# Attention, gated MLP and MLP on one core: both heads' scores of a query tile issued in turn, in the first batch

## The chip, the cores and the metric

The kernel runs on one core of a Trainium2 chip. The metric is the device time of one execution in microseconds (us). Engines are called by their names or as the profile does: PE is TensorE (PEld its weight loads), DVE is VectorE, ACT is ScalarE, POOL is GpSimd, SP is SyncE, which issues most DMAs.

## The reference

Block-causal attention (4 batches, 8 heads, 576 positions, head dimension 64, blocks of 64), then a gated MLP with a spatial product over the positions, then a normalized MLP with a residual. The change lies in the attention's first product, the scores.

```python
scores = scale * np.matmul(q, k.transpose(0, 1, 3, 2))
scores = np.where(mask, scores, -1000000000.0)
attn = np.exp(scores - np.max(scores, axis=-1, keepdims=True))
attn = attn / (np.sum(attn, axis=-1, keepdims=True) + 1e-09)
x = np.matmul(attn, v)
...
h = np.maximum(x @ w_in, 0.0)
...
gated = u * v_s
x = gated @ w_out
...
ch = np.maximum(xn @ w_ch1, 0.0) @ w_ch2
return (x + ch).astype(np.float32)
```

## The kernel before

The attention works on **pairs** of heads, 4 pairs a batch, pairs 0 to 15. A pair is cut into 7 **units** in the order of `UNITS`: the tail (the last 64 query rows of both heads in one tile of 128 rows, `c == 4`), then the query tiles 3, 2 and 1 (128 rows each; tile 1 also takes tile 0 along), each for head 0 and then for head 1. In the text 3/0 is tile 3 of head 0, 3/1 that of head 1, and so on. The main loop (`for u in range(NS + 8)`) takes one unit after another through three stages:

- `scores(u)`: matmuls into a PSUM bank of the pool `p_sc`, which has three banks. q and k are held as a high and a low part that sum to the fp32 value (`stacks`, and `qtail` for the tail). In the first batch (pairs below `PACKED` = 4) head 0 lies on partitions 0 to 63 and head 1 on 64 to 127, and a score is three products over 64 rows: high by high, high by low, low by high. From pair 4 on a score is two products over 128 rows. The first three units (`PLAIN`) take the fp32 operands as they are.
- `softmax(u)`: VectorE adds the mask, takes the minimum and writes the tile `p` to SBUF in one reduction (L322), which frees the score bank; ScalarE does the exponential and the sum (L328). There are six `p` tiles (`pt`) and a single `tail` tile.
- `transposes(u - 2)`: TensorE turns the probabilities, 128 columns at a time (L378), into one of two banks of `p_tr`, and VectorE or ScalarE copies them to `pH` or `pL` (L370, L372).

`weighted` then multiplies with v (pv, L429), in a first half on `pL` and a second one on `pH`; `reciprocals` (rps, L341, and the copy rr, L343) and `store_x` finish a pair. In between stand `prepare` (high and low parts of a later pair: L56 or L58 for the high ones, on GpSimd L233 or L245 and L247 for the low ones), the decoding of w_in (`DECODE`: ACT L88, DVE L89 and L90, POOL L101 and L102) and, from pair 4 on, the first dense matmuls (vps, ups: L106 to L108) which `fill` adds.

The order on each engine is not that of the source: the kernel is built with a scheduler that keeps a time line of its own and moves instructions within what their data allow. `tc.keep_in_program_order` (here `pin`) holds the instructions it is given in the order of the source among themselves. The zero matmuls of `warm` and of `lead` (`ZEROS`) are extra work for TensorE; `lead` writes them into a score bank before the scores.

```python
ZEROS = {NU * p + i: n for p in range(4) for i, n in ((6, 1), (7, 2))}
...
UNITS = [(None, 4)] + [(j, c) for c in (3, 2, 1) for j in range(2)]
...
elif p < PACKED:
    for i, (x, y) in enumerate(((0, 0), (0, 1), (1, 0))):
        MM(out, lhsT=st[rows, x, 0, q], rhs=st[rows, y, 1, 0:nn], start=(i == 0), stop=(i == 2))
```

Of the kernel before, what the change touches and what calls it, by code (L numbers as in the profile page):

```python
# [8 lines left out]
F32 = mybir.dt.float32  # L9
# [24 lines left out]
def tile_kernel(  # L34
# [35 lines left out]
    MM = nc.tensor.matmul  # L70
# [62 lines left out]
    p_sc = tc.alloc_tile_pool(name="p_sc", bufs=PLAN["sc"], space=PSUM, side="right")  # L133
# [7 lines left out]
    PACKED = PLAN['packed']  # L141
# [26 lines left out]
    def pin(ins, on=True):  # L168
        if on:
            tc.keep_in_program_order(ins)  # L170
# [85 lines left out]
    NU = len(UNITS)  # L256
    PLAIN = PLAN['plain']
    state = {}

    sums = {}  # L260

    ZEROS = {NU * p + i: n for p in range(4) for i, n in ((6, 1), (7, 2))}

    def scores(u):
        p = u // NU
        j, c = UNITS[u % NU]

        def lead(ps):
            for _ in range(ZEROS.get(u, 0)):
                MM(ps, lhsT=zeros.to_broadcast([128, 128]), rhs=zeros.to_broadcast([128, 512]), start=True, stop=True)  # L270
        st, qt, _, raw = ops[p]
        banks = []
        plain = u < PLAIN
        if c == 4:
            sums[p] = at.tile([128, 9], F32, tag="sm", name="sm")
            for a, z in ((0, 256), (256, S)):
                s_ps = p_sc.tile([128, 512], F32, tag="sc", name="sc")
                if a == 0:
                    lead(s_ps)
                if plain:  # L280
                    pin(MM(s_ps[:, :z - a], lhsT=last_q, rhs=raw[:, 0, 1, a:z], start=True, stop=True))
                elif p < PACKED:
                    for n, (x, y) in enumerate(((0, 0), (0, 1), (1, 0))):
                        MM(s_ps[:, :z - a], lhsT=qt[:, x, 0, :], rhs=st[:, y, 1, a:z], start=(n == 0), stop=(n == 2))
                else:
                    for h in range(2):
                        for i in range(2):
                            MM(  # L288
                                s_ps[:, :z - a], lhsT=qt[:, i, h, :], rhs=st[:, h, 2, a:z],
                                start=(h == 0 and i == 0), stop=(h == 1 and i == 1),  # L290
                            )
                banks.append((s_ps[:, :z - a], a, z - a))
        else:
            s_ps = p_sc.tile([128, 512], F32, tag="sc", name="sc")
            lead(s_ps)
            rows = slice(64 * j, 64 * j + 64) if j is not None else None
            for a, c in ((0, c),) if c > 1 else ((0, 1), (256, 0)):
                n = 128 * (c + 1)
                out = s_ps[:, a:a + max(n, 192)]
                nn = max(n, 192)  # L300
                q = slice(128 * c, 128 * c + 128)
                if plain:
                    pin(MM(out, lhsT=raw[rows, 0, 0, q], rhs=raw[rows, 0, 1, 0:nn], start=True, stop=True))
                elif p < PACKED:
                    for i, (x, y) in enumerate(((0, 0), (0, 1), (1, 0))):
                        MM(out, lhsT=st[rows, x, 0, q], rhs=st[rows, y, 1, 0:nn], start=(i == 0), stop=(i == 2))
                else:
                    for i in range(2):
                        MM(out, lhsT=st[:, j, i, q], rhs=st[:, j, 2, 0:nn], start=(i == 0), stop=(i == 1))  # L309
                banks.append((s_ps[:, a:a + n], 0 if c != 1 else 128, n))  # L310
        state[u] = banks

    def softmax(u):
# [245 lines left out]
    for u in range(NS + 8):  # L559
        p, i = divmod(u, NU)  # L560
        if u < NS:
            scores(u)
            warm(WARM.get(u, 0))
            softmax(u)
# [624 lines left out]
```

## Time and profile before

| what | value |
|---|---|
| median of 3 runs | 796.72 us (794.71 to 797.81) |
| the profiled execution | 793.98 us |
| its span, first to last instruction | 792.2 us |
| PE busy | 776.4 us, 98% of the span |
| DVE, ACT, POOL busy | 513.9, 428.6, 419.2 us |
| granted TensorE clock, mean | 1.000 |
| units 0 to 27, the first batch | up to about 51.7 us, where the tail scores of pair 4 begin |

A busy time is the union of an engine's instructions. For PE the ends of matmuls are modelled and they overlap, so the step from one start to the next start tells more than a duration. The value in brackets behind a row of the timeline is the engine's idle time ahead of it and what ended it.

### The profile page before, as it was taken

How to read it: one execution, taken by the hardware profiler on the slowest of the kernel's cores; microseconds unless marked ns; L12 is line 12 of the kernel's file. 1: busy time of each engine (PE TensorE's matmuls, PEld its weight loads, DVE VectorE, ACT ScalarE, POOL GpSimd, SP SyncE). 2: the span in 40 equal slices, each digit the busy share in tenths (PEclk: the TensorE clock that was granted, in tenths of full speed). 3: DMA queues.
4: the chain of work that ended last, by engine and by line, in shares of the span. 5: the costliest groups of instructions: out<-in, count | busy, mean ns of one | idle time of the engine just before them, and what ended most of it. 6: DMA issues, size and time to landing. Idle time of an engine off the chain costs nothing.

```text
span 792.2 us, 13259 instructions
## 1 busy us (share of the span) xinstructions
PE 776.4 (98%) x4508; PEld 669.4 (84%) x4508; DVE 513.9 (65%) x1165; ACT 428.6 (54%) x1051; POOL 419.2 (53%) x436
## 2 busy tenths in 40 slices
PE   9999999999999999899999999999999999999997
PEld 5766788778888899789988988889989898898996
DVE  6677756555464457786777788897566588555534
ACT  5888776777654464555444555553354454333421
POOL 5699966675632453232375565465545465545431
PEclk9999999999999999999999999999999999999999
DMA  9866455545332669779420332204010003000002
GB/s 251 206 177 171 126 173 154 154 119 154 96 115 74 197 199 289 224 247 285 135 81 24 110 107 82 80 19 141 1 30 25 0 1 125 23 0 1 1 1 79
DMA packets 53847, 88.70 MB, mean 112 GB/s; under 512 B 6930, under 2 KB 17298, under 8 KB 53780
## 3 DMA queue, kind: packets, MB, share of 16 engines
q1 hardware_dynamic: 53540, 87.55, 37.2%
q8 instruction: 35, 0.57, 0.3%
q10 hardware_dynamic: 240, 0.31, 0.2%
q14 instruction: 32, 0.26, 0.1%
HBM read 68.88 MB, written 18.95 MB: 111 GB/s over the span
## 4 chain that ended last, share of the span: by engine, by line
PE 86%; DVE 6%; DMA 3%; issue 2%; POOL 1%; ACT 1%; SPq 1%; DVEq 0%; ACTq 0%; POOLq 0%
PE hps L968 21%; PE o L106 8%; PE o L107 8%; PE o L108 8%; PE pv L429 6%; PE tr L378 4%; PE sc L309 3%; PE ups L106 2%; PE vps L106 2%; PE ups L108 2%; PE ups L107 2%; PE vps L107 2%; PE vps L108 2%; PE sc L288 2%; PE by L106 2%
## 5 line engine op out<-in xcount | busy, mean ns | idle before, releaser
L102 POOL TENSOR_TENSOR a<-s,a 128x256 fp32r<-128x256 f32 x96 | 78.2, 818 | 91.4 <-ACT a L97 91.4
L107 PE MATMUL o<-w,h 128*128 128x512 f32 x288 | 112.3, 391 | 0.0
L106 PE MATMUL o<-w,h 128*128 128x512 f32 x288 | 107.0, 395 | 1.0 <-ACT h L960 1.0
L974 DVE TENSOR_TENSOR c<-hps,c 128x384 f32<-128x384 f32 x120 | 66.5, 554 | 52.1 <-PE hps L968 50.5
L108 PE MATMUL o<-w,h 128*128 128x512 f32 x288 | 96.5, 394 | 0.3 <-DVE h L961 0.3
L102 POOL TENSOR_TENSOR a<-w,a 128x256 fp32r<-128x256 f32 x72 | 61.5, 856 | 44.3 <-ACT a L97 38.5
L97 ACT CAST a<-s 128x256 fp32r<-128x256 f32 x96 | 38.3, 404 | 83.4 <-PE hps L968 74.9
L328 ACT ACTIVATE p<-p,nm 128x512 f32<-128x512 f32 (+3 forms) x128 | 70.9, 556 | 18.1 <-DVE nm L322 14.5
L322 DVE CUSTOM_DVE_ANT_0 p<-sc,mask 128x512 f32<-128x512 f32 (+3 forms) x128 | 58.3, 484 | 33.2 <-PE tr L378 12.5
L106 PEld LDWEIGHTS o<-w,h 128*128 128x128 f32 x288 | 53.8, 188 | 11.0 <-ACT h L960 2.3
L107 PEld LDWEIGHTS o<-w,h 128*128 128x128 f32 x288 | 54.1, 188 | 9.6
L370 DVE COPY pH<-tr 128x512 f32<-128x512 f32 (+1 forms) x88 | 49.2, 575 | 19.7 <-PE tr L378 19.4
L108 PEld LDWEIGHTS o<-w,h 128*128 128x128 f32 x288 | 53.2, 188 | 8.4 <-DVE h L961 1.2
L818 POOL TENSOR_TENSOR gt<-gf,gt 128x576 fp32r<-128x576 f32 (+1 forms) x17 | 25.0, 1472 | 62.5 <-ACT gt L817 62.5
L378 PE MATMUL tr<-idn,p 128*128 128x128 f32 x320 | 48.8, 276 | 2.1 <-DVE pH L370 1.9
L439 POOL TENSOR_TENSOR xx<-xx,rb 128x576 f32<-128x576 f32 x16 | 22.7, 1421 | 49.1 <-DMA rb<-r_d 40.3
L961 DVE SCALAR_TENSOR_TENSOR h<-c,h 128x384 fp32r<-128x384 f32 x72 | 46.0, 658 | 1.6 <-ACT h L960 1.5
L88 ACT ACTIVATE dm<-raw 128x256 f32<-128x256 f32 (+1 forms) x72 | 31.8, 462 | 27.4 <-DVE w L90 6.3
L378 PEld LDWEIGHTS tr<-idn,p 128*128 128x128 f32 x320 | 36.9, 140 | 10.6 <-DVE pH L370 5.3
L309 PE MATMUL sc<-stack 128*128 128x256 f32 (+2 forms) x192 | 42.7, 338 | 2.9 <-DVE nm L322 2.5
L245 POOL TENSOR_TENSOR stack<-qkt,stack 64x576 fp32r<-64x576 f32 x24 | 34.0, 1417 | 21.4 <-ACT stack L58 15.8
L117 POOL TENSOR_TENSOR rs<-rs,nhalf 128x1 f32<-128x1 f32 x36 | 22.4, 622 | 42.6 <-DVE rs L116 37.0
(188 smaller groups left out, 2270.7 us busy)
## 6 DMA issues: line engine op xcount, KB each, us to landing
raw<-in_w_ch_dram SPq DMA_DIRECT2D x64, 256.0 KB
qkt<-in_qk_dram SPq DMA_DIRECT2D x110, 144.0 KB
vt<-in_v_dram SPq DMA_DIRECT2D x16, 320.0 KB
rb<-r_d SPq DMA_DIRECT2D x32, 144.0 KB
u_d<-ur SPq DMA_DIRECT2D x16, 288.0 KB
us<-u_d SPq DMA_DIRECT2D x16, 288.0 KB
y_d<-ys SPq DMA_DIRECT2D x18, 256.0 KB
yr<-y_d SPq DMA_DIRECT2D x18, 256.0 KB
```

What stands on the lines that cost most here:

```text
L102: {"v": nc.vector, "g": nc.gpsimd}[low].tensor_tensor(lo, src, f32(hi), op=ALU.subtract)
L106: MM(out_ps, lhsT=a[0], rhs=b[0], start=first, stop=False)
L107: MM(out_ps, lhsT=a[0], rhs=b[1], start=False, stop=False)
L108: MM(out_ps, lhsT=a[1], rhs=b[0], start=False, stop=last)
L309: MM(out, lhsT=st[:, j, i, q], rhs=st[:, j, 2, 0:nn], start=(i == 0), stop=(i == 1))
L322: nc.vector.tensor_tensor_reduce(pt[:, o:o + n], src, m, -0.125, nm[:, 0:1] if c == 4 and i == 1 else 3e38, ALU.add, ALU.min, nm[:, i:i + 1],)
L328: nc.scalar.activation(pt[:, o:o + n], pt[:, o:o + n], AF.Exp, bias=nm[:, i:i + 1], scale=-1.0, accum_out=sm[:, col:col + 1])
L370: nc.vector.tensor_copy(out, src)
L378: nc.tensor.transpose(tr[:, o:o + 128], pt[:, 128 * kc:128 * kc + 128], idn)
L429: MM(ps[64 * j:64 * j + 64, a:z], lhsT=vt[:rows, kc, 64 * j:64 * j + 64], rhs=src[:rows, j, w * kc + a:w * kc + z] if part else src[:rows, ...
L968: MM(ps, lhsT=a[x], rhs=b[y], start=not more and kc == 0 and k == 0, stop=kc == KD // 2 - 1 and k == 2, skip_group_check=True,)
L974: nc.vector.tensor_tensor(out, ps, x, op=ALU.add)
```

## The change

In the first batch, behind the three plain units, `scores` is done for both heads of a tile when head 0's unit comes: two banks are taken, one for each head, and the three products are issued in turn, head 0, head 1, head 0 and so on. All but the first of these matmuls are pinned in the source's order. Head 1's unit then finds its state filled and issues no scores. The single zero matmul of `lead` moves from unit 6 (1/1) to unit 5 (1/0) of a pair, so that it comes ahead of tile 1's scores. For the tail, the plain units and the pairs from 4 on the same matmuls are issued as before.

```diff
-    ZEROS = {NU * p + i: n for p in range(4) for i, n in ((6, 1), (7, 2))}
+    ZEROS = {NU * p + i: n for p in range(4) for i, n in ((5, 1), (7, 2))}
...
-            s_ps = p_sc.tile([128, 512], F32, tag="sc", name="sc")
-            lead(s_ps)
...
-                elif p < PACKED:
-                    for i, (x, y) in enumerate(((0, 0), (0, 1), (1, 0))):
-                        MM(out, lhsT=st[rows, x, 0, q], rhs=st[rows, y, 1, 0:nn], start=(i == 0), stop=(i == 2))
...
+            parts = ((0, c),) if c > 1 else ((0, 1), (256, 0))
+            heads = (0, 1) if p < PACKED and not plain else (j,)
+            if j == heads[0]:
+                pss = {h: p_sc.tile([128, 512], F32, tag="sc", name="sc") for h in heads}
+                lead(pss[j])
+                for a, c in parts:
...
+                    terms = ((0, 0), (0, 1), (1, 0)) if p < PACKED else ((0, 2), (1, 2))
+                    for i, (x, y) in enumerate(terms):
+                        for h in heads:
+                            rows = slice(64 * h, 64 * h + 64)
+                            left, right = (st[rows, x, 0, q], st[rows, y, 1, 0:nn]) if p < PACKED else (
+                                st[:, h, x, q], st[:, h, 2, 0:nn])
+                            ins = MM(
+                                pss[h][:, a:a + nn], lhsT=left, rhs=right, start=(i == 0), stop=(i == len(terms) - 1)
+                            )
+                            pin(ins, len(heads) > 1 and (i > 0 or h > 0 or a > 0))
+                for h in heads:
+                    state[u + h - j] = [
+                        (pss[h][:, a:a + 128 * (c + 1)], 0 if c != 1 else 128, 128 * (c + 1)) for a, c in parts
+                    ]
+            return
```

The scheduler makes its order anew from this. The queues of all five engines differ up to the first scores of pair 8 (about 114 us of the profile) and list the same instructions in the same order from there on. In the changed kernel the lines behind the edit are higher by 10: L312 are these scores, L332 the reduction, L380 the pH copy, L388 the transposes, L439 pv.

TensorE in pair 2, tiles 3 and 2, before (sc_501 and sc_525 are the banks of 3/0 and 3/1, sc_551 and sc_567 of 2/0 and 2/1):

```order
L306 MATMUL sc_501<-stack0_89 128x512 x3
L378 MATMUL tr_385<-idn_114,p_330 128x128 x4
L306 MATMUL sc_525<-stack0_89 128x512 x3
L378 MATMUL tr_400<-idn_114,p_354 128x128 x4
L306 MATMUL sc_551<-stack0_89 128x384 x3
L378 MATMUL tr_420<-idn_114,p_380 128x128 x3
L306 MATMUL sc_567<-stack0_89 128x384 x3
```

and with the change (sc_501 and sc_502 are now 3/0 and 3/1, sc_551 and sc_552 2/0 and 2/1):

```order
L312 MATMUL sc_501<-stack0_89 128x512
L312 MATMUL sc_502<-stack0_89 128x512
L312 MATMUL sc_501<-stack0_89 128x512
L312 MATMUL sc_502<-stack0_89 128x512
L312 MATMUL sc_501<-stack0_89 128x512
L312 MATMUL sc_502<-stack0_89 128x512
L388 MATMUL tr_400<-idn_114,p_354 128x128 x4
L388 MATMUL tr_428<-idn_114,p_384 128x128 x3
L312 MATMUL sc_551<-stack0_89 128x384
L312 MATMUL sc_552<-stack0_89 128x384
```

The transposes that stood between two heads of a tile now stand behind both.

TensorE in pair 3 before, from the transposes of pair 2's tail on (sc_676 and sc_703 are the banks of 3/0 and 3/1; pv_544 is the first half of pair 1's pv, on pL):

```order
L378 MATMUL tr_533<-idn_114,tail_122 128x128 x4
L306 MATMUL sc_676<-stack1_90 128x512 x3
L306 MATMUL sc_703<-stack1_90 128x512 x3
L378 MATMUL tr_541<-idn_114,tail_122 128x128
L429 MATMUL pv_544<-pL_363,vt_134 64x256 x2
L429 MATMUL pv_544<-pL_363,vt_134 64x128 x2
```

and with the change (sc_676 and sc_677 are 3/0 and 3/1):

```order
L388 MATMUL tr_533<-idn_114,tail_122 128x128 x4
L312 MATMUL sc_676<-stack1_90 128x512
L388 MATMUL tr_541<-idn_114,tail_122 128x128
L439 MATMUL pv_544<-pL_363,vt_134 64x256 x2
L439 MATMUL pv_544<-pL_363,vt_134 64x128 x2
L312 MATMUL sc_677<-stack1_90 128x512
L312 MATMUL sc_676<-stack1_90 128x512
L312 MATMUL sc_677<-stack1_90 128x512
```

The first matmul of the tile, which is not pinned, stands alone, and other work comes between it and the other five. The same holds for tiles 2 and 1 of this pair.

VectorE in pair 1 before (p_380 and p_396 are the reductions of 2/0 and 2/1, p_414 the first one of 1/0, dm and de the decoding of w_in, rr the copy of the reciprocals):

```order
L89 TENSOR_SCALAR de_254<-raw_170 128x512
L322 ISA p_380,nm_381<-sc_376,mask_119 128x384
L322 ISA nm_381 128x1
L89 TENSOR_SCALAR de_342<-raw_172 128x512
L90 SCALAR_TENSOR_TENSOR dm_253<-dm_253,de_254 128x512
L343 COPY rr_317<-rps_315 9x128
L322 ISA p_396,nm_397<-sc_392,mask_119 128x384
L322 ISA nm_397 128x1
L322 ISA p_414,nm_415<-sc_407,mask_119 128x256
```

and with the change (p_384, p_396 and p_422 are the same three reductions):

```order
L89 TENSOR_SCALAR de_262<-raw_170 128x512
L90 SCALAR_TENSOR_TENSOR dm_261<-dm_261,de_262 128x512
L89 TENSOR_SCALAR de_346<-raw_172 128x512
L353 COPY rr_317<-rps_315 9x128
L332 ISA p_384,nm_385<-sc_376,mask_119 128x384
L332 ISA nm_385 128x1
L332 ISA p_396,nm_397<-sc_377,mask_119 128x384
L332 ISA nm_397 128x1
L380 COPY pH_364<-tr_358 128x4x2x64
L90 SCALAR_TENSOR_TENSOR dm_345<-dm_345,de_346 128x512
L332 ISA p_422,nm_423<-sc_407,mask_119 128x256
```

The first L90 and the copy rr now stand ahead of both reductions of tile 2, and the pH copy and the second L90, which stood behind the reductions of tile 1, ahead of them.

## Rows read from the trace of the kernel before

**Rows 1.** The page, part 4: the chain of waits by engine, over the whole span.
```profile
PE 86%; DVE 6%; DMA 3%; issue 2%; POOL 1%; ACT 1%; SPq 1%; DVEq 0%; ACTq 0%; POOLq 0%
```

**Rows 2.** Windows cut at the first scores of pairs 2, 3 and 4.
```profile
core 0: us, PE busy (x) PEld busy (x) DVE busy (x) ACT busy (x) POOL busy (x), PEclk, DMA share, GB/s
...
25.10:37.50 12.40, 12.40 (x82) 8.26 (x81) 8.44 (x27) 8.97 (x31) 9.08 (x10) 1.00 0.95 221
37.50:51.70 14.20, 13.39 (x93) 9.40 (x91) 10.41 (x30) 12.26 (x32) 13.75 (x14) 1.00 0.64 175
```

**Rows 3.** Timeline of PE in pair 2: start, us, engine, line, operation, count.
```profile
27.98 0.66 PE L378 MATMUL tr<-idn,p 128*128 128x128 f32 x4
28.57 0.96 PE L306 MATMUL sc<-stack 64*128 64x512 f32 x3
29.46 0.66 PE L378 MATMUL tr<-idn,p 128*128 128x128 f32 x4
...
30.77 0.55 PE L378 MATMUL tr<-idn,p 128*128 128x128 f32 x3
...
31.96 0.55 PE L378 MATMUL tr<-idn,p 128*128 128x128 f32 x3
...
36.40 0.93 PE L306 MATMUL sc<-stack 64*128 64x256 f32 x6
37.27 0.61 PE L270 MATMUL sc<-const-float32-0.0 128*128 128x512 bf16 x2
```

**Rows 4.** Timeline of PE: a lone score matmul (pair 1), and eight transposes unbroken (pair 4).
```profile
22.42 0.55 PE L378 MATMUL tr<-idn,p 128*128 128x128 f32 x3
22.90 0.35 PE L306 MATMUL sc<-stack 64*128 64x192 f32 x1
23.18 0.39 PE L270 MATMUL sc<-const-float32-0.0 128*128 128x512 bf16 x1
...
55.41 1.03 PE L378 MATMUL tr<-idn,p 128*128 128x128 f32 x8
56.20 0.59 PE L309 MATMUL sc<-stack 128*128 128x384 f32 x2
```

**Rows 5.** Timeline of PE in pair 1: 3/0 and 3/1 together.
```profile
17.16 0.97 PE L306 MATMUL sc<-stack 64*128 64x512 f32 x6
18.06 0.55 PE L378 MATMUL tr<-idn,p 128*128 128x128 f32 x3
```

**Rows 6.** Timeline of PE in pair 0: end of 2/1, then 1/0.
```profile
11.07 0.62 PE L306 MATMUL sc<-stack 64*128 64x384 f32 x2
11.62 0.61 PE L177 MATMUL idle<-const-float32-0.0 128*128 128x512 bf16 x2
12.16 0.81 PE L306 MATMUL sc<-stack 64*128 64x256 f32 x5
12.90 0.39 PE L177 MATMUL idle<-const-float32-0.0 128*128 128x512 bf16 x1
```

**Rows 7.** Windows, columns as in rows 2: parts of pairs 2 and 3.
```profile
28.00:33.20 5.20, 5.20 (x30) 3.62 (x29) 4.60 (x17) 2.87 (x8) 3.06 (x5) 1.00 0.88 211
38.60:48.80 10.20, 9.39 (x61) 6.32 (x61) 10.02 (x28) 8.85 (x23) 9.83 (x9) 1.00 0.59 181
```

**Rows 8.** Timeline of DVE: both L90 of pair 1, and two reductions.
```profile
21.00 0.69 DVE L90 SCALAR_TENSOR_TENSOR dm<-dm,de 128x512 uint32<-128x512 uint32 x1 [0.18 <-ACT dm L88]
...
26.75 1.33 DVE L90 SCALAR_TENSOR_TENSOR dm<-dm,de 128x512 uint32<-128x512 uint32 x1
28.00 0.41 DVE L322 CUSTOM_DVE_ANT_0 tail<-sc,mask 128x256 f32<-128x256 f32 x1
...
38.58 0.42 DVE L322 CUSTOM_DVE_ANT_0 p<-sc,mask 128x256 f32<-128x256 f32 x1 [1.79 <-PE tr L378]
```

**Rows 9.** Timeline of PE: the stalls of pairs 3 and 5.
```profile
46.12 0.55 PE L378 MATMUL tr<-idn,p 128*128 128x128 f32 x3 [0.75 <-DVE pH L370]
...
74.93 0.71 PE L309 MATMUL sc<-stack 128*128 128x256 f32 x4 [1.65 <-DVE nm L322]
```

More of the change, by code (lines that the diff above doesn't have):

```diff
@@ L293, in scores @@
         else:
-            s_ps = p_sc.tile([128, 512], F32, tag="sc", name="sc")
-            lead(s_ps)
[L296 to L303, printed above, removed]
-                elif p < PACKED:
-                    for i, (x, y) in enumerate(((0, 0), (0, 1), (1, 0))):
-                        MM(out, lhsT=st[rows, x, 0, q], rhs=st[rows, y, 1, 0:nn], start=(i == 0), stop=(i == 2))
[L307 to L310, printed above, removed]
+            parts = ((0, c),) if c > 1 else ((0, 1), (256, 0))
@@ new lines, in scores @@
+            heads = (0, 1) if p < PACKED and not plain else (j,)
[3 more added lines that the diff above has]
+                for a, c in parts:
+                    nn = max(128 * (c + 1), 192)
+                    q = slice(128 * c, 128 * c + 128)
+                    if plain:
+                        rows = slice(64 * j, 64 * j + 64)
+                        pin(MM(pss[j][:, :nn], lhsT=raw[rows, 0, 0, q], rhs=raw[rows, 0, 1, 0:nn], start=True, stop=True))
+                        continue
+                    terms = ((0, 0), (0, 1), (1, 0)) if p < PACKED else ((0, 2), (1, 2))
[12 more added lines that the diff above has]
+                    ]
```

## Prediction

> **What bounds the kernel now.** I read the chain of waits first. TensorE carries 86% of it [rows 1], so a shorter TensorE stream could shorten the run, wherever nothing else takes over. Next come the windows cut at the pairs. In pair 2 (25.1 to 37.5 us) TensorE is busy in all 12.40 us, in pair 3 in 13.39 of 14.20 [rows 2]. The granted clock is 1.00, the 2.4 GHz level, in each. TensorE is thus the bound of the stretch that is edited, but not by far: in 38.6 to 48.8 us VectorE is busy for 10.02 of 10.20 us and GpSimd for 9.83 [rows 7]. A saving on TensorE will therefore run into VectorE's queue, and most of the work below is to see how much of it comes through.
>
> The timeline of TensorE then gives the price of a "visit", one head's scores of a tile with the change of array shape before and after. From the transposes ahead of 3/1 to those behind it, 27.98 to 29.46, pass 1.48 us [rows 3]. Eight transposes in an unbroken row take 56.20 - 55.41 = 0.79 [rows 4], four of them 0.40. The visit costs 1.08. In the same way 2/1 costs (31.96 - 30.77) - 0.30 = 0.89, and 1/1 costs 37.27 - 36.40 = 0.87 [rows 3], with about 0.1 for its way in 0.97. A lone matmul of 192 columns between transposes and zeros costs (23.18 - 22.42) - 0.30 = 0.46 [rows 4]. A lone one buys almost nothing: most of that is the two changes of shape.
>
> Do two heads run side by side? In pair 1 the six 512-column matmuls of 3/0 and 3/1 stand together, from 17.16 until the transposes at 18.06: 0.90 us [rows 5]. In pair 2 the three of 3/1 alone take 29.46 - 28.57 = 0.89 [rows 3]. The second head was free, although the order lists head 0's three ahead of head 1's three. The Trainium skill (TensorE: Matmul & The Clock Gate, Part 3, The mechanism) says that matmuls start and end strictly in program order and are not reordered. By that rule the six would have taken about 0.9 + 0.7 us (0.89 less the change of shape), and the change would still gain that 0.7 on this pair. The trace disagrees: it is already taken there, and I count none.
>
> **The change part by part.** Counts of matmuls, their columns, the zero matmuls and all DMAs stay; only order changes, up to about 114 us. From the ups matmul at that point on, all five queues list the same instructions in the same order. So the gain is what has been won by then, and TensorE is the chain's carrier afterwards [rows 1].
>
> TensorE, if nothing else held it:
> - Pair 0: the last two matmuls of 2/1 (11.07 to 11.62, 0.55) run beside 2/0's, and the rest of 1/0 (12.16 to 12.90, 0.74) beside 1/1's [rows 6]: 1.3 us.
> - Pair 1: five visits before and after; two streams more run side by side. An estimate of 0.3, between 0 and one merged visit of 0.89.
> - Pair 2: three visits of head 1 go (1.08 + 0.89 + 0.97 = 2.94), the lone first matmul of 1/0 comes (0.46): 2.5 us.
> - Pair 3: the new order cuts off the first matmul in all three tiles and splits the last once more. Tile 3, which ran partly side by side, gains nothing; tile 2 gains 0.89 - 0.46 = 0.43, tile 1 0.97 - 2 x 0.46 = 0.05: 0.5 us.
>
> Sum 4.6 us, the ceiling of the matmul part. Two stalls could add to it: 0.75 at 46.1 us, behind VectorE's pH copies, and 1.65 at 74.9 us, behind a reduction [rows 9]. The new order puts two value matmuls (vps, some 0.23 us each, an estimate from 512 columns: 0.89 / 3 less a share of the shape change) into the place of the second: 0.45 us. The ceiling is 4.6 + 0.75 + 0.45 = 5.8.
>
> What of it passes VectorE? I follow its reductions (L322), each of which frees a score bank.
> - Pair 0: between 0 and 1.3 us. The zero matmuls stand as gaps on TensorE there, so reductions come sooner when scores do; I let two thirds through, 0.9.
> - Pair 1: the new order moves both L90 of the w_in decoding, and the pH copy of the tail, ahead of the reductions of tiles 2 and 1. L90 took 0.69 at one place and 1.33 at another [rows 8]. The second, at 26.75 before, stood behind them. From 0.9 + 0.3 I take off 0.7, about the short form: the first reduction of pair 2 comes 0.5 us sooner than at 28.00 [rows 8]. The bounds are 0 (long form) and 1.2 (hidden).
> - Pair 2: TensorE saves 2.5, but VectorE was busy 4.60 of the 5.20 us that follow [rows 7], so only about 0.5 passes. Then 1/1's reduction, at 38.58, waits for TensorE's transposes [rows 8], those of pair 1's last tile, whose p buffer it reuses. They now stand behind the second-half pv, rps and the second score bank of pair 3's tail, so they cannot use the rest. I take 0.9 at this point, sum so far.
> - Pair 3: VectorE is full from there to 48.8 [rows 7]. The 0.9 stays, and the pH stall with it. At the end one matmul of 1/0 stands ahead of pv and the other eleven behind it, where 1/1 alone stood: with its shape changes, 0.5 more. 1.4 at the start of pair 4.
> - Pairs 4 and 5: in pair 4 the transposes of the old tail come before the new tail's second bank, and both passes of tile 1 ahead of pv. That saves one or two changes of shape, about 0.3 each (the lone matmul's 0.46 less its own columns) [rows 4]: 0.5. The two vps in the stall give 0.45, rounded down to 0.4.
>
> Sum 0.9 + 0.5 + 0.5 + 0.4 = 2.3 us. SP's and POOL's queues carry the same work in another order: POOL does a second w_in piece before pair 3's low halves, and pair 4's halves in one run. I cost this at nothing: between 28.0 and 33.2 us GpSimd was busy for 3.06 of 5.20 us [rows 7], and these 2.1 us of holes hide the earlier piece. Without that cover pair 4's halves, and pair 5's behind them, come late by as much, and so do their first scores.
>
> Profiled time 793.98 less 2.3 is 791.7. That execution lies 2.74 us under the median of 796.72, so the forecast is **794.4 us**.
>
> **Rivals.**
> *The whole saving comes through.* VectorE has holes (0.60 of 5.20 us at 28 us) [rows 7], its decoding operations can fall into them, and the two stalls can close; then 796.7 - 5.8 = 790.9. Against it: the full window behind 38.6. Chance 0.15.
> *Nothing is left.* VectorE and GpSimd set the pace from 38 us on (10.02 and 9.83 of 10.20) [rows 7], and what TensorE wins it waits for at 46 and 75 us: 796.7, within 1 us. The Trainium skill (TensorEngine Tiling (Array Packing), Performance Considerations, PSUM Bottleneck) speaks for this: tiling speeds up TensorE and not the emptying of its banks. No number above rests on it. Chance 0.23.
> *Slower, by the head of VectorE's queue.* In pair 1 the first L90 now stands ahead of both reductions of tile 2, and behind the arrival and decoding of a w_in piece, while the DMA engines were 0.95 busy in pair 2 [rows 2]. It decides if that piece is decoded later than the scores of tile 2, some 21 us. From there every us late is one lost: a long L90 twice (1.33 - 0.69 = 0.64 each) eats 1.3 of the 2.3, and a piece 2.5 us late makes 796.7 + 1.5 = 798.2. Chance 0.11.
> *The change does not do what it says*: matmuls in turn do not run side by side, each exposing its weights. Then pair 1 loses the 0.9 it has, and the merged visits give only their changes of shape back: 797. The row of 0.90 for six [rows 5] speaks against it. Chance 0.03.
> The forecast keeps 0.48.
>
> **How the numbers follow.** A measurement of this kernel can tell about 0.5% from no change, 4.0 us. Faster than 792.7 are the first rival and 0.04 of the forecast's upper bounds (0.7 more in pair 1, the 0.75 stall, 0.4 in pair 2): 0.19. Slower than 800.7 needs the third rival with a piece 5 us late: 0.04. Same: 0.77. The range goes from the first rival's 790.9 to the third's 798.2; outside it I leave about half of the first and a part of the third and of the spread of runs (794.71 to 797.81), under 0.2.
>
> **What would show it.** Pair 2's passes of tiles 3 and 2 each last as long as one head's (0.9 us for tile 3). The first reduction of pair 2 comes about 0.5 us before 28.0, that of 1/1 at about 37.7 for 38.58, pair 4's tail scores start near 50.3 for 51.67. Behind 114 us everything is shifted by one amount. Wrong it would be if the six of a pair last 1.3 us or more, if pair 2 begins later than 25.1, if the stalls at 46 and 75 us grow by what was saved, or if the clock falls below 1.00 in a stall.

## The result and the profile after

The changed kernel takes **801.51 us** (median of 9 runs, 797.22 to 802.34), the kernel before beside it 795.28 (9 runs, 793.77 to 797.81): a ratio of 1.0062 [1.0047, 1.0077], in brackets the 95% interval, here and below. By the ratio that is 4.9 us slower (by the medians 6.2), where 2.3 us faster was forecast, and it is outside the range of 790.9 to 798.2. The profiled execution took 799.57 us with a span of 797.8 us and a mean granted clock of 0.993; before it was 793.98, 792.2 and 1.000. In both kernels the longer runs tend to be those with the lower mean clock; that is taken up below.

The scores do run side by side. Timeline of PE in pairs 1 and 2 of the changed kernel, columns as in [rows 3]:

```profile
16.29 1.13 PE L312 MATMUL sc<-stack 64*128 64x512 f32 x6
17.35 0.55 PE L388 MATMUL tr<-idn,p 128*128 128x128 f32 x3
...
29.74 0.93 PE L312 MATMUL sc<-stack 64*128 64x384 f32 x6
30.60 0.55 PE L388 MATMUL tr<-idn,p 128*128 128x128 f32 x3
```

Both heads of tile 2 of pair 2 take 0.86 us, about what one head's visit took in [rows 3], and both of tile 3 of pair 1 take 1.06 (0.90 in [rows 5], where head 0's three were listed first). Yet windows cut as in [rows 2] and continued show TensorE less busy in pair 3, and a mean clock below 1.00 in each window from there on (by windows of 2 us in two spells, between 44 and 54 us and between 78 and 84). TensorE's share of the chain of waits, 86% in [rows 1], is 82% on the page after, and DMA's 5% for 3%:

```profile
PE 82%; DMA 5%; DVE 5%; POOL 2%; ACT 2%; SPq 2%; issue 2%; ACTq 0%; POOLq 0%; DVEq 0%
```

The windows:

```profile
core 0: us, PE busy (x) PEld busy (x) DVE busy (x) ACT busy (x) POOL busy (x), PEclk, DMA share, GB/s
25.10:37.50 12.40, 11.52 (x88) 7.88 (x85) 7.97 (x28) 10.60 (x33) 7.21 (x7) 1.00 0.87 224
37.50:51.70 14.20, 9.67 (x48) 5.85 (x48) 7.76 (x24) 7.94 (x24) 13.66 (x14) 0.78 0.57 164
51.70:65.00 13.30, 13.18 (x98) 9.32 (x97) 8.44 (x27) 10.44 (x29) 11.07 (x9) 0.98 0.52 136
65.00:81.00 16.00, 14.04 (x91) 9.94 (x89) 11.91 (x38) 13.01 (x31) 14.41 (x12) 0.95 0.74 181
81.00:98.00 17.00, 16.64 (x99) 12.34 (x95) 10.10 (x30) 9.08 (x24) 13.78 (x15) 0.94 0.53 141
```

Where it is lost shows best in the start of each pair's rps matmul (the last of a pair's attention), taken from the timeline of PE, one profiled execution in each row:

| kernel | pair 0 | 1 | 2 | 3 | 4 | 5 |
|---|---|---|---|---|---|---|
| before | 21.45 | 36.20 | 49.79 | 62.76 | 77.77 | 94.86 |
| before, second profile (base) | 21.98 | 36.71 | 49.85 | 62.78 | 78.20 | 95.48 |
| changed | 20.40 | 36.14 | 53.51 | 67.32 | 83.25 | 101.04 |
| changed, second profile (again) | 20.85 | 36.59 | 54.58 | 69.65 | 85.42 | 102.98 |
| hold | 20.33 | 36.07 | 46.82 | 61.89 | 78.87 | 96.86 |
| rb | 20.00 | 35.72 | 52.42 | 66.22 | 79.79 | 98.83 |
| holdrb | 20.50 | 36.23 | 48.24 | 62.56 | 79.74 | 97.24 |
| hold2 | 20.23 | 35.96 | 47.72 | 62.03 | 74.70 | 98.00 |
| hold5 | 20.27 | 36.00 | 48.02 | 63.08 | 75.96 | 93.85 |
| hold5, second profile (hold5b) | 20.16 | 35.91 | 47.70 | 62.78 | 75.65 | 93.68 |

The two profiles of the kernel before differ by up to 0.62 us in these columns, those of the changed kernel by up to 2.33. In the changed kernel everything is lost between 36 and 101 us; later pairs keep the distance (pair 15: 261.42 for 255.27). The largest piece lies in pair 3. Timeline of PE there:

```profile
41.51 0.44 PE L312 MATMUL sc<-stack 64*128 64x384 f32 x1
45.97 0.90 PE L388 MATMUL tr<-idn,p 128*128 128x128 f32 x3 [4.02 <-DVE pH L380]
46.80 1.33 PE L312 MATMUL sc<-stack 64*128 64x384 f32 x5
48.05 1.54 PE L388 MATMUL tr<-idn,p 128*128 128x128 f32 x6
...
50.46 3.12 PE L439 MATMUL pv<-pH,vt 128*64 128x320 f32 x20
```

Tile 2's first matmul starts at 41.51, 1.4 us ahead of the 42.90 of before. Then the stall of 0.75 us of [rows 9] has become 4.02 us, and what follows it is slow: twenty pv matmuls need 3.12 us here and 2.27 before. Why it stalls is read engine by engine, following each releaser. The changed kernel's timeline of VectorE:

```profile
45.15 0.21 DVE L349 RECIPROCAL sm<-sm 128x9 f32<-128x9 f32 x1 [4.95 <-ACT sm L348]
45.28 0.63 DVE L380 COPY pH<-tr 128x512 f32<-128x512 f32 x1
```

Its timeline of ScalarE:

```profile
44.51 0.40 ACT L249 CAST qtail<-stack 128x256 fp32r<-128x256 f32 x1 [4.33 <-POOL stack L245]
44.82 0.30 ACT L348 ACTIVATE sm<-sm,tiny 128x9 f32<-128x9 f32 x1
45.02 0.76 ACT L338 ACTIVATE tail<-tail,nm 128x576 f32<-128x576 f32 x1
```

And of GpSimd:

```profile
35.27 1.42 POOL L449 TENSOR_TENSOR xx<-xx,rb 128x576 f32<-128x576 f32 x1 [4.82 <-ACT stack L58]
...
43.09 1.39 POOL L245 TENSOR_TENSOR stack<-qkt,stack 64x576 fp32r<-64x576 f32 x1
```

TensorE waits for VectorE's pH copy. That stands behind the reciprocal, which waits for ScalarE's sum copy (L348). That in turn stands behind L249, the copy of **pair 4's** query tail, which waits for GpSimd's second low half of pair 4 (L245). The Trainium skill (TensorE: Matmul & The Clock Gate, Part 1, Architectural detail) calls ScalarE's and VectorE's queues strict FIFO. The rows agree: the sum copy started 44.82, as soon as L249 let it. Before, L249 stood behind the sum copy (L338) and pair 3's tail exponential (L328), and there nothing waited behind it. The timeline of ScalarE before:

```profile
42.19 0.31 ACT L338 ACTIVATE sm<-sm,tiny 128x9 f32<-128x9 f32 x1
42.76 0.78 ACT L328 ACTIVATE tail<-tail,nm 128x576 f32<-128x576 f32 x1 [0.27 <-DVE nm L322]
...
43.65 0.41 ACT L249 CAST qtail<-stack 128x256 fp32r<-128x256 f32 x1
```

GpSimd itself is late, since its product with rb started at 35.27. Before:

```profile
32.59 1.42 POOL L439 TENSOR_TENSOR xx<-xx,rb 128x576 f32<-128x576 f32 x1 [2.14 <-DMA rb<-r_d]
```

The row of after puts the wait down to ScalarE's cast L58. That cast is not what it waits for: in the run hold below, GpSimd has the same list and starts this product at 32.69, ahead of that cast (34.05), and in the second profile of the changed kernel the row names the DMA of rb. The timeline of SP's issues points to a cause, which the run rb tests:

```profile
26.01 0.33 SPq L166 DMA_DIRECT2D vt<-in_v_dram  x1
29.03 1.11 SPq L358 DMA_DIRECT2D rb<-r_d  x2
```

The load of a v stands ahead of rb, the broadcast of pair 0's reciprocals. Before, rb was ahead of that load:

```profile
27.40 1.11 SPq L348 DMA_DIRECT2D rb<-r_d  x2
28.60 0.54 SPq L166 DMA_DIRECT2D vt<-in_v_dram  x1
```

A second stall comes on TensorE in pair 5, in the place where [rows 9] had 1.65 us behind a reduction, and pv is slow again behind it:

```profile
78.26 0.50 PE L106 MATMUL vps<-win,xT 128*128 128x512 f32 x1 [1.84 <-POOL xT L60]
...
79.36 3.96 PE L439 MATMUL pv<-pH,vt 128*64 128x320 f32 x20
```

### The profile page after: what moved, and what is told of

Read it like the earlier page. It is cut to its first block, busy times and chain, and to the rows that moved or that the text cites. A ratio compares the mean times of both kernels' runs of the same rounds, so it can differ in the third digit from the quotient of the medians.

```text
span 797.8 us, 13261 instructions
## 1 busy us (share of the span) xinstructions
PE 777.6 (97%) x4504; PEld 668.3 (84%) x4508; DVE 509.2 (64%) x1165; ACT 428.7 (54%) x1051; POOL 418.2 (52%) x436
## 4 chain that ended last, share of the span: by engine, by line
PE 82%; DMA 5%; DVE 5%; POOL 2%; ACT 2%; SPq 2%; issue 2%; ACTq 0%; POOLq 0%; DVEq 0%
PE hps L978 21%; PE o L106 8%; PE o L107 8%; PE o L108 8%; PE pv L439 6%; PE tr L388 4%; PE sc L312 3%; PE ups L106 2%; PE vps L106 2%; PE ups L108 2%; PE ups L107 2%; PE vps L107 2%; PE vps L108 2%; DMA qkt<-in_qk_dram 2%; PE by L106 2%
## 5 line engine op out<-in xcount | busy, mean ns | idle before, releaser
L338 ACT ACTIVATE p<-p,nm 128x512 f32<-128x512 f32 (+3 forms) x128 | 70.9, 557 | 13.7 <-DVE nm L332 11.5
L332 DVE CUSTOM_DVE_ANT_0 p<-sc,mask 128x512 f32<-128x512 f32 (+3 forms) x128 | 57.8, 483 | 30.1 <-PE sc L312 11.5
L380 DVE COPY pH<-tr 128x512 f32<-128x512 f32 (+1 forms) x88 | 49.0, 574 | 20.1 <-PE tr L388 20.1
L312 PE MATMUL sc<-stack 128*128 128x192 f32 (+7 forms) x282 | 56.4, 345 | 2.2 <-DVE nm L332 1.6
L388 PE MATMUL tr<-idn,p 128*128 128x128 f32 x320 | 49.3, 281 | 4.9 <-DVE pH L380 4.7
L388 PEld LDWEIGHTS tr<-idn,p 128*128 128x128 f32 x320 | 37.2, 142 | 14.2 <-DVE pH L380 8.5
L312 PEld LDWEIGHTS sc<-stack 128*128 128x128 f32 (+1 forms) x282 | 38.0, 190 | 12.2 <-DVE nm L332 6.0
L245 POOL TENSOR_TENSOR stack<-qkt,stack 64x576 fp32r<-64x576 f32 x24 | 34.4, 1432 | 25.5 <-ACT stack L58 20.2
```

The costliest lines, as they stand in the source:

```text
L312: ins = MM(pss[h][:, a:a + nn], lhsT=left, rhs=right, start=(i == 0), stop=(i == len(terms) - 1))
L332: nc.vector.tensor_tensor_reduce(pt[:, o:o + n], src, m, -0.125, nm[:, 0:1] if c == 4 and i == 1 else 3e38, ALU.add, ALU.min, nm[:, i:i + 1],)
L338: nc.scalar.activation(pt[:, o:o + n], pt[:, o:o + n], AF.Exp, bias=nm[:, i:i + 1], scale=-1.0, accum_out=sm[:, col:col + 1])
L380: nc.vector.tensor_copy(out, src)
L388: nc.tensor.transpose(tr[:, o:o + 128], pt[:, 128 * kc:128 * kc + 128], idn)
```

## The experiments

Theory 1, from these rows: an instruction that waits at the head of a queue (L249 on ScalarE, the v load on SP, later the value matmuls on TensorE) takes the gain, and the clock behind each stall takes more. Theory 2: the two banks, the lone matmuls and the new order of the scores cost the time themselves. Theory 3: only GpSimd's lateness counts. Each time is the median of 5 to 12 runs, and each ratio is to the kernel before, run in the same group on the same chip. `issue_after(x)` queues what it encloses behind x on x's engine and moves nothing else by itself.

**hold.** One instruction moves on ScalarE; all other queues list what they did.

```diff
+            if p == PACKED:
+                held.enter_context(tc.issue_after(exps[NU * (p - 1)].ins))
+                held.enter_context(tc.issue_after(sms[p - 2].ins))
...
             nc.scalar.copy(
                 view(qt, 0, [[192, 2], [256, 2], [1, 64]]), f32(view(st, 512, [[3 * S, 2], [S, 2], [1, 64]]))
```

> The changed kernel with one instruction moved: ScalarE's copy of pair 4's query tail (L249) is held behind pair 2's sum copy and pair 3's tail exponential; every other queue and the rest of ScalarE's list as in the changed kernel. Theory 1 (that copy, waiting for GpSimd's low halves at the head of ScalarE's queue, is what stops VectorE and then TensorE): the stall of 4.02 us of TensorE ahead of the transposes at 45.97 us shrinks to under 1.2 us, the granted clock stays 1.00 there, pair 2's reciprocals (rps) come at 48.3 to 49.8 us in place of 53.51, and the time falls by 4 to 7 us from the changed kernel's 801.5, to 794.5 to 797.5. Theory 2 (the order of the scores on TensorE, with its lone matmuls and two banks taken at once, costs the time by itself): a stall of about the same length at another place, time within 1.5 us of 801.5. Theory 3 (GpSimd's lateness, from the v load ahead of the reciprocals' broadcast on SyncE's queue, is what counts, and pair 4's tail scores wait for it in any case): the stall moves to the tail scores of pair 4, time 800 to 801.5.

798.09 us, 1.0026 [1.0009, 1.0042]. The stall of 4.02 is gone: the same three transposes start at 41.85 with no wait, and pair 2's rps comes at 46.82, 2.97 us **ahead** of before (and ahead of the range). That speaks against theory 2: TensorE's list is the same, and no stall of that length came at this place or ahead of it. But the median missed its range by 0.6 us. The profiled execution, at 795.36 us the fastest of the twelve, lies inside the range, so it does not show why; what it shows is the next loss, in pair 5, where the second stall has grown to 2.65 us. The timeline of PE in hold:

```profile
41.85 0.55 PE L394 MATMUL tr<-idn,p 128*128 128x128 f32 x3
...
44.62 2.27 PE L445 MATMUL pv<-pH,vt 128*64 128x320 f32 x20
...
73.98 0.58 PE L106 MATMUL vps<-win,xT 128*128 128x512 f32 x1 [2.65 <-POOL xT L60]
...
75.71 3.23 PE L445 MATMUL pv<-pH,vt 128*64 128x320 f32 x20
```

Not all of what pair 2 won is the moved row's. In this execution rb also landed sooner, although SP's list is the same: GpSimd's product starts at 32.69 (35.27 in the changed kernel), and L245 of pair 4 ends at 42.29 (44.48). The timeline of ScalarE in hold parts the two:

```profile
39.99 0.32 ACT L354 ACTIVATE sm<-sm,tiny 128x9 f32<-128x9 f32 x1
...
42.33 0.41 ACT L253 CAST qtail<-stack 128x256 fp32r<-128x256 f32 x1 [1.23 <-POOL stack L245]
```

The sum copy starts 4.83 us sooner than the 44.82 of the changed kernel. Behind this L249 it would have started at 42.33 + 0.31 = 42.64 (0.31 as from 44.51 to 44.82): by this estimate 2.65 us are the order's, 2.18 GpSimd's.

The run also gives the **price of the clock**. TensorE lists the same instructions in both kernels. From these transposes to rps pass 46.82 - 41.85 = 4.97 us here, without a stall, and 53.51 - 45.97 = 7.54 us in the changed kernel, also without one. So of the 6.69 us between the two rps, 4.12 are the wait and **2.57 the slower work behind it**; in pair 5 of the changed kernel pv to rps takes 3.89 us for the 2.20 of before, 1.69 more. The windows of the changed kernel, every 2 us, tell the level:

```profile
42.00:44.00 2.00, 0.00 (x0) 0.00 (x0) 0.00 (x0) 0.00 (x0) 1.93 (x2) 1.00 0.75 218
44.00:46.00 2.00, 0.03 (x1) 0.04 (x1) 0.85 (x3) 1.37 (x4) 1.87 (x2) 0.85 0.02 8
46.00:48.00 2.00, 2.00 (x8) 1.28 (x8) 2.00 (x7) 1.10 (x3) 1.91 (x4) 0.50 0.31 78
```

TensorE had been idle since 41.9 us, the clock fell to 0.50 (1.2 GHz), and it was back at 0.95 in 52 to 54 us.

**rb.** One transfer moves on SP.

```diff
+            if p == 3:
+                held.enter_context(tc.issue_after(rb_dma[0].ins))
             last_load[:] = [nc.sync.dma_start(out=vts[p], in_=v[divmod(p, NP)])]
```

> The changed kernel with one transfer moved: the load of pair 3's v is issued behind the broadcast of pair 0's reciprocals (rb) on SyncE's queue, as before the change; every other queue as in the changed kernel. Theory 1: rb lands up to 1.6 us sooner (issued about 27.4 for 29.03 us), GpSimd's product at 35.27 and all that follows it on GpSimd moves by 1 to 2 us, and the stall of 4.02 us shrinks by as much, to 2 to 3 us; time 798.5 to 800.5. Theory 3: with GpSimd on time the stall goes altogether, time below 797.5. Theory 2: no change in the time, 801 to 802.

796.97 us, 1.0003 [0.9984, 1.0021]: lower than theory 1 said, and in the range of theory 3. rb is issued no sooner (29.12 us), so that part of the expectation missed; but without the load ahead of it GpSimd's product starts at 33.58, 1.69 us sooner. The profiled execution, at 799.22 us the slowest of the 12, still shows 3.30 us of stall (theory 1 said 2 to 3, theory 3 none), so how long it lasts in a common run of this kernel is not seen. The intervals of hold and rb overlap: which of the two edits is worth more stays open. The two waits are in series, since the copy waits for GpSimd. So the time alone would fit theory 3, but the profiles speak against it: with that low half ended at 43.33 TensorE stalls for 3.30 us while L249 is ahead, and with it ended at 43.62 for 0.75 in the kernel before and 1.31 in hold5 (below), where L249 is behind. The second profile of the kernel before (base, below) says it most clearly. There GpSimd is later than in the changed kernel, L245 of pair 4 ends at 45.11, and TensorE waits 0.65 us. The timelines of GpSimd and of PE in base:

```profile
43.70 1.41 POOL L245 TENSOR_TENSOR stack<-qkt,stack 64x576 fp32r<-64x576 f32 x1
...
45.98 0.87 PE L378 MATMUL tr<-idn,p 128*128 128x128 f32 x6 [0.65 <-ACT pH L372]
```

GpSimd's lateness thus costs where L249 stands ahead of others, and not by itself.

**holdrb.** Both edits.

> Both of the edits above together. Theory 1: within 1 us of the run that moves the copy alone, since GpSimd's lateness has nothing queued behind it any more (the stall of 1.84 us at 76.4 us, behind GpSimd's copy to xT, may shrink and give up to 1 us more). Theory 3: 2 us or more below the run that moves the copy alone.

796.47 us, 1.0006 [0.9991, 1.0021], 1.6 us below hold and so between the two expectations. Pair 2's rps comes at 48.24 (before 49.79), with the clock at 1.00; in pair 5 TensorE waits 3.00 us for xT (0.89 in rb), and pv is slow behind it as in hold. So against rb alone no difference is shown: in the profile what pair 3 won went in pair 5. The timeline of SP in holdrb shows why xT is late: r_d, the reciprocals on their way to be broadcast, stands behind eight loads.

```profile
59.52 4.98 SPq L160 DMA_DIRECT2D qkt<-in_qk_dram  x8
64.59 0.66 SPq L364 DMA_DIRECT2D r_d<-rr  x1
```

From pair 3's rps at 62.56 to the issue of r_d pass 2.03 us; before it was 0.62 (62.76 to 63.38). GpSimd's product with rb then waits 1.23 us for it, at 72.27.

**nopin.** The pins go; the heads' matmuls then stand three and three.

```diff
-                            pin(ins, len(heads) > 1 and (i > 0 or h > 0 or a > 0))
```

> The changed kernel without its pins: both heads' scores are still traced in turn into two banks, but the scheduler orders them freely (it puts head 0's matmuls ahead of head 1's, in most tiles next to each other, in some with transposes between), and it leaves pair 4's query tail copy behind pair 2's sum copy and pair 3's tail exponential by itself. Theory 1: no stall above 2 us before 60 us, clock 1.00, time 793 to 797. Theory 2: the two banks taken at once cost by themselves, time 799 or more.

796.60 us, 0.9997 [0.9978, 1.0017]: within the range for the time, but the "no stall above 2 us" failed. L249 is behind the tail exponential and ahead of the pH copies now, GpSimd is later still (L245 ends at 46.28, for 44.48), and the same wait comes back one place on: TensorE stalls for 3.80 us at 47.15, and the clock is 0.50 in 46 to 52 us. So the time came true without the reason that was given for it. What this profile has less of is the loss behind: in pair 5 TensorE waits 1.57 us for a reduction, as before the change, and not for xT, the clock stays at 1.00 there, and pair 5's rps comes at 97.87 (101.04 in the changed kernel). The timeline of ScalarE in nopin:

```profile
46.31 0.40 ACT L249 CAST qtail<-stack 128x256 fp32r<-128x256 f32 x1 [4.53 <-POOL stack L245]
46.62 0.47 ACT L381 COPY pH<-tr 128x384 f32<-128x384 f32 x1
```

**again.** The changed kernel, no edit.

> The changed kernel once more, as it is, beside the others of this group on one chip. By the earlier runs 1.0062 of the kernel before; theory 1 expects 800 to 802.5, the stall of some 4 us at 42 to 46 us again and the granted clock at 0.50 behind it.

800.46 us, 1.0059 [1.0041, 1.0078]. The second profile has a stall of 3.65 us at 46.03, then the clock at 0.50, and one of 1.39 us at 80.14.

**hold2.** holdrb, and the last value matmuls of the first value tile behind pair 4's rps.

```diff
+                if pair == 0 and t == 0 and kc == KD - 1:
+                    held.enter_context(tc.issue_after(rps_ins[PACKED].ins))
                 mm3(
```

> Three edits of the queues of the changed kernel: ScalarE's query tail copy (L249) of pair 4 behind the sum copy and the tail exponential, the v load of pair 3 behind rb, and the last three value matmuls of the first value tile (vps, which wait for pair 3's xT) behind pair 4's reciprocals, where they stood before the change. Theory 1 in full (three waits at the head of a queue take the whole gain, and the fall of the clock behind them as much again): no stall of TensorE above 1.7 us before 95 us, the clock 1.00 in the profiled run, pair 4's reciprocals at 75.3 to 76.5 us (77.77 before, 79.74 with two of the edits), time 1.5 to 3 us below the kernel before, ratio 0.996 to 0.998. Theory 4 (VectorE is full in pairs 3 and 4, so TensorE waits for a reduction instead of for xT): a stall of 2 us or more behind a reduction between 71 and 76 us, ratio 0.999 to 1.002.

Pair 4's rps comes at 74.70, 3.07 us ahead of before and better than forecast; the stall behind xT is down to 0.83 us (at 76.28, behind those reciprocals). Yet the kernel takes 797.52 us, 1.0025 [1.0013, 1.0037], and both theories missed: a fourth wait stands ahead of pair 5's pv, and the clock falls again. The timeline of PE in hold2:

```profile
93.75 4.32 PE L450 MATMUL pv<-pH,vt 128*64 128x320 f32 x20 [2.86 <-ACT p L346]
```

ScalarE's:

```profile
91.87 0.60 ACT L508 ACTIVATE vr<-vps 128x512 f32<-128x512 f32 x1 [0.75 <-DMA vn_d<-vr]
92.36 0.71 ACT L346 ACTIVATE p<-p,nm 128x512 f32<-128x512 f32 x1
```

And VectorE's:

```profile
92.50 0.69 DVE L112 BATCH_NORM_STATS2 st<-vr 128x6 f32<-128x512 f32 x1 [2.37 <-ACT vr L508]
93.11 0.54 DVE L391 COPY pH<-tr 128x384 f32<-128x384 f32 x1
```

The scheduler put the third value tile's relu (L508) ahead of two exponentials, and its statistics (L112) ahead of a pH copy; the relu waits until an earlier value tile is stored.

**hold5.** hold2, and that relu behind the two exponentials.

```diff
+        if u == NU * 6 + 2:
+            tc.add_manual_dep(
+                relu[0, 2].ins, exps[u].ins.name,
...
```

> The run with three edits of the queues, and a fourth: ScalarE's relu of the third value tile (which waits for a vr buffer to be stored, and behind which two exponentials of pair 6 and VectorE's pH copy stand) is held behind those exponentials. Theory 1: the stall of 2.86 us ahead of pv at 93.75 us goes, and the clock stays 1.00 to 110 us; pair 5's reciprocals at 91.5 to 93.5 us (94.86 before, 98.00 with three edits), time 792.5 to 795, ratio 0.997 to 0.9995. Theory 4 (whatever TensorE wins, some queue behind it takes): another stall of 2 us or more, ratio 1.000 to 1.003.

**794.22 us, 0.9963 [0.9946, 0.9980]**: faster than both kernels. The ratio is just below the range of theory 1, pair 5's rps comes at 93.85 (0.35 later than the range), no stall before 100 us is longer than 1.31 us, and the clock is 1.00 in every window of 6 us from 36 to 108 us. The four orders that it holds are those in which the kernel before lists these instructions, so none of them is a gain of its own. With the fourth edit the scheduler also listed some later instructions anew (another relu and its statistics, three transposes, some ups matmuls, a v load, all between 95 and 108 us), so the win over the kernel before is not the change's alone beyond doubt.

**hold5b.** The same once more.

> The run with four edits of the queues once more, as it is, since it was picked from several. Theory 1: ratio to the kernel before 0.9945 to 0.9985 again, mean clock 0.998 or more. If the first result was luck: 0.999 to 1.001.

793.08 us, 0.9967 [0.9950, 0.9985]. It holds, with a mean clock of 0.9985 over its runs.

**zeros.** The kernel before with the zero matmul alone moved, `((6, 1), (7, 2))` to `((5, 1), (7, 2))`.

> The kernel before with one part of the change alone: the single zero matmul moves from unit 6 to unit 5 of a pair. The scheduler then puts the v load of pair 3 ahead of rb, as in the changed kernel, but leaves ScalarE's copy where it was. Theory 1: a stall of 1 to 3 us near 46 us behind a pH copy, time 0 to 2.5 us above the kernel before. A theory by which the side by side scores themselves cost the time expects no difference here, within 0.5 us.

796.65 us, 1.0007 [0.9993, 1.0021]: no difference is shown, and theory 1's stall of 1 to 3 us did not come (0.77 us, at 47.65). The v load is ahead of rb here too and L245 of pair 4 ends at 45.14, but L249 has its old place and TensorE itself is 1.3 us later at pair 1's rps (37.50), so the run says little about how late the changed kernel's GpSimd is. What it does say: SP's new order, with L249 in its old place, cost nothing that this run shows. That no difference came is also what the other theory expected; hold5, which keeps the scores side by side and is faster, speaks against that one.

**pinall.** The first matmul of a tile pinned as well: `pin(ins, len(heads) > 1)`.

> The changed kernel with the first matmul of a tile pinned too, so that no lone matmul stands apart from the other five. ScalarE's copy then stands behind the sum copy and the tail exponential and the two pH copies ahead of it. The prediction's price of a lone matmul (0.46 us, five or six of them in pairs 2 and 3) would give 2 to 2.5 us; theory 1 expects no stall above 2 us at 42 to 47 us and 793.5 to 796.5 in all. Against it: pinning holds each tile behind everything traced ahead of it, so TensorE may wait for reductions in pairs 1 to 3, then 797 or more.

803.13 us, 1.0104 [1.0090, 1.0118]. Pair 1's rps comes at 30.61 (the scheduler also lists it earlier), but theory 1 missed here too: a stall of 2.50 us came at 41.68, behind a pH copy of ScalarE, and later a value matmul waits for pair 3's xT at the head of TensorE's queue, 5.76 us, by the timeline of PE in pinall:

```profile
70.44 0.80 PE L108 MATMUL vps<-win,xT 128*128 128x512 f32 x1 [5.76 <-POOL xT L452]
```

The price of a lone matmul could not be read from it.

**warm24.** The changed kernel with `ZEROS[NU * 3 + 3] = 16`.

> The changed kernel with 16 zero matmuls of 512 columns more, written into the bank of tile 2 of pair 3 ahead of its scores, that is into the place where TensorE stood idle for 4 us; ScalarE's query tail copy stays ahead of pair 2's sum copy, as in the changed kernel. At the full clock they take 16 x 0.21 = 3.4 us. Clock theory (half or more of the loss is the granted clock at 0.50 behind the stall, and the runs with a mean clock near 1.000 take 794 to 795 us whatever the kernel): TensorE is kept busy, the clock stays 1.00 between 42 and 54 us, pair 2's reciprocals come at 50 to 51.5 us (53.51 and 54.58 in the two profiles of the changed kernel), time 796.5 to 798.5, some 3 us below the changed kernel though TensorE does 3.4 us more work. Against it (the wait alone counts, the clock little): time 800.5 to 804.

The timeline of PE in warm24:

```profile
41.38 3.66 PE L271 MATMUL sc<-const-float32-0.0 128*128 128x512 bf16 x15
44.98 0.44 PE L313 MATMUL sc<-stack 64*128 64x384 f32 x1
45.73 0.55 PE L389 MATMUL tr<-idn,p 128*128 128x128 f32 x3 [0.31 <-DVE pH L381]
```

Most of the local part came true: the transposes start at 45.73, the clock is 1.00 in 42 to 54 us, and the tail scores of pair 4 start at 53.05 for 55.48, with 16 more matmuls ahead of them; pair 2's rps, at 52.69, missed its 50 to 51.5. The time did not come true: 800.63 us, 1.0047 [1.0031, 1.0063], which is in the range of the theory against it. The scheduler listed the later matmuls anew, and at 61.47 us a stall of 1.72 us follows, with a clock of 0.72 in 60 to 66. So in this profile the clock stayed up where the stall was filled; the run does not settle the clock's share of the whole.

**base.** The kernel before against itself.

> The kernel before, once more, unchanged: a comparison of it with itself, for the spread, and a second profile of it. The profile that the prediction was made from had a mean clock of 1.000, while the median of 62 runs of that kernel lies near 0.997. Clock theory: a profiled run below 1.000 shows one of the known stalls (46, 59, 75 or 92 us) followed by some microseconds at 0.50, and takes 1 to 4 us more than 793.98; the runs lie on one line, about 0.5 to 0.9 us for each 0.001 of mean clock. Ratio 0.998 to 1.002.

796.03 us, 0.9995 [0.9978, 1.0011]. The second profile had a clock of 1.000 too, so it does not show where that kernel's clock falls in a common run.

## Why the prediction was wrong

**Right.** Side by side: as above. The milestones up to 41 us held: pair 0 gained 1.05 us at its rps (0.9 forecast for its reductions); the first reduction of pair 2 came at 27.47 (0.5 before 28.00 forecast); the reduction of 1/1 at 37.34 (37.7). The last half us of these is within what two profiles of the kernel before differ by (28.00 and 28.52 for that first reduction). Behind 114 us all is shifted by nearly one amount (rps 6.17 us later in pair 6, 6.15 in pair 15). With the queues put right, the size of the sum, 2.3 us, comes out as well: hold5 lies 796.38 - 794.22 = 2.2 us below the kernel before by the medians, and 3.4 in its repeat (2.9 and 2.6 by the ratios). That is partly luck. The forecast took the clock as equal, and hold5's is higher; among the runs with a mean clock of 0.999 or more the medians are 792.9 (13 runs) and 794.6 (25), which leaves 1.7 us. And by the first scores of pair 8, where all was to be won, the two profiles of hold5 stand at 113.80 and 113.63, those of the kernel before at 114.18 and 114.81: 0.4 to 1.2 us. The tail scores of pair 4, forecast near 50.3, start between 48.80 and 50.21 in hold, holdrb, hold5 and its repeat. So a gain of this order was there in TensorE's stream, how it divides among the prediction's terms is not measured, and the changed kernel's time is set by its queues.

**The step that failed first**: "SP's and POOL's queues carry the same work in another order ... I cost this at nothing ... these 2.1 us of holes hide the earlier piece." Those holes were not free time. Before, GpSimd had waited in them for rb (2.14 us ahead of 32.59), and rb now goes out 1.6 us later and behind a v load; the hole became 4.82 us, and pair 4's second low half (L245) ended 0.86 us later (44.48 for 43.62). Undoing SP's order alone brought the time back from 1.0062 to 1.0003 (rb), so it was not worth nothing. The record speaks for a cost only together with the second step: in zeros the v load is ahead of rb too, L249 is in its old place, and the ratio is 1.0007; in base the same L245 ended at 45.11, later than here, with a stall of 0.65 us. How late it is differs by execution: with that order of SP the product with rb starts between 32.69 and 35.79 in five profiles of the changed kernel and its variants, with rb ahead between 32.26 and 34.00 in seven (35.23 in zeros and 31.91 in pinall, which list more in another order, are left out). The step's own condition, "come late by as much, and so do their first scores", also looked one place too far: it was not the scores of pair 4 that waited first, but the copy L249.

**The second**: "Pair 3: VectorE is full from there to 48.8. The 0.9 stays, and the pH stall with it." VectorE was not full, it stood still for 4.95 us behind ScalarE. ScalarE's queue was in no term. The new order lists L249 ahead of the sum copy and the tail exponential, one row that moved, with GpSimd behind it; hold undoes that row, and the stall and the lower clock behind it are gone. The price of the wait was 4.02 us, where the prediction let 0.75 stand. The rival "slower, by the head of VectorE's queue" had the right mechanism on the wrong engine, and with 1.5 us a third of the size.

**The third**: "The two vps in the stall give 0.45". The stall of [rows 9] at 75 us lay behind a reduction, and the value matmuls put there wait for pair 3's xT: 1.84, 1.39, 2.65 and 3.00 us (changed, again, hold, holdrb). A matmul is a filler only if its operands are there.

**The fourth, and the size**: the clock stood in the prediction's last line ("or if the clock falls below 1.00 in a stall") and in no sum. Over the runs of this study the changed kernel has a mean clock of 0.993 (21 runs), the one before 0.997 (118), hold5 0.9985 (22). A line through the changed kernel's 21 runs gives 0.85 us for each 0.001: 4 x 0.85 = 3.4 us of the 5 us; the line through the 118 runs of the kernel before gives 0.56, which makes it 2.2. Both are estimates from runs that differ in their stalls too, so there is no clean split. The prediction also worked from one profile with a clock of 1.000 and carried its 2.74 us under the median along without asking where they come from; 25 of those 118 runs have 0.999 or more, and their median is 794.6.

What stays open: the shares of L249 and of rb, and where the clock of the kernel before falls in a common run.

## What to carry to other kernels

When a planner makes its order anew, go through every queue for instructions of a **later** stage that now stand ahead of one somebody is waiting for, and ask what each waits for; the gain of the edited engine says nothing about that. Idle time before an engine's instruction is cover only if nothing that ends it has moved: look at its releaser first. And price a TensorE stall of some microseconds at more than its length, since the work behind it may run at half the clock.

## What the hardware showed unexpectedly

The clock does not always fall behind a stall of the same place and length. Far from the change, at 330 us, every kernel waits for VectorE's yn. In the profiled execution of the kernel before, 2.49 us of it left the clock at 1.00; in hold5's, 2.20 us were followed by 0.51 in 330 to 332 us, and the same four transposes took 1.05 us for 0.63. Of the fourteen profiles here three lost the clock at that place, after 2.20, 1.90 and 1.90 us (hold5, rb, hold2), and eleven did not, after 0.84 to 2.49. The timeline of PE in the kernel before:

```profile
330.43 0.63 PE L751 MATMUL ytr<-idn,yn 128*128 128x128 f32 x4 [2.49 <-DVE yn L122]
```

And in hold5:

```profile
330.01 1.05 PE L781 MATMUL ytr<-idn,yn 128*128 128x128 f32 x4 [2.20 <-DVE yn L122]
```

In pair 5, too, stalls of 1.84 and 1.39 us were followed by the lower clock in the two profiles of the changed kernel, while 2.04 us in the kernel before (75.36 us of its second profile) were not. The Trainium skill (TensorE: Matmul & The Clock Gate, Part 1, What's actually happening) says that the monitor behind the clock runs freely and does not start with the kernel, so that its effect differs from run to run; these rows agree that it differs, and do not show why. The price of a short stall thus varies; the stalls of 3.3 to 4.0 us were followed by the lower clock in all four profiles that had one.
